# Row-half copies of weight differences on the compute engines, other stores from SyncE, and another order of a hand-ordered opening

## The chip, the cores and the metric

The kernel runs on one core of a Trainium2 chip. The metric is device microseconds of one execution; the median of five runs is quoted. A run is profiled separately, and every start time below is counted from the start of the profiled span of the kernel before.

The engines are named as in the profile: PE is TensorE, with PEld for its weight loads, DVE is VectorE, ACT is ScalarE, POOL is GpSimd and SP is SyncE. SP computes nothing here; it issues DMAs.

## The reference

There are two stages. The first is a dynamic convolution over time: each of 8 heads has 7 logits per position, a softmax turns them into weights, and each position's 192 features become the weighted sum of the last 7 positions' features. The second is a maxout layer over the 33,280 resulting rows.

```python
w = np.exp(weight_gen - weight_gen.max(-1, keepdims=True))     # (8, 4160, 8 heads, 7 taps)
w = w / (w.sum(-1, keepdims=True) + 1e-09)
out = np.einsum('bshk,bskhg->bshg', w, x_unf)                  # x_unf: 7 causal taps of x, zero padded
x = out.reshape(33280, 192)
g = np.maximum(x @ w1, x @ w2)                                 # w1, w2: (192, 1024)
return g @ w_out                                               # (1024, 192)
```

## The kernel before, in words

**The maths as the kernel does it.** Since max(a, b) = a + relu(b − a), the kernel forms d = w2 − w1 once, computes relu(x·d)·w_out on PE and adds x·(w1·w_out), where w1·w_out (tile `w10`, 192×192) is also formed once. The softmax is exp, a sum, a logarithm, a subtraction in place in the logits, and a second exp that writes the weights (`en_t`) in bf16.

**Tiling.** Each of the 128 partitions holds 260 consecutive positions, called columns. Columns come in batches of 16 (16 whole batches and one of 4). A batch is cut into units: the first batch into four units of 4 columns, the others into units of 8. DVE multiplies x by the weights (`mul`, L186, into `m_t`) and adds the seven taps (`add`, L203 and L208, into `y_t`). A DMA transpose issued by SP (L223) turns a unit's rows into features by tokens (`yt`). For the first two batches PE itself adds and transposes the taps (`tap_sums`, L261) and an engine copies the result to `yt` (`features`, L274). Then hidden tiles: 128 hidden features by 1024 tokens (`hid_tile`, L304: pairs of matmuls over 64 partition rows), relu to bf16 (`rd_t`, L318), and products with `w_out` into PSUM (`out_first`, L362, with `w10`; `out_hidden`, L350), a copy to `o_t` (`evac`, L406) and a store (L420).

**The weight differences.** The 192 feature rows are held as 128 rows (kind E) and two times 64 (kind T). Tile `wd` has three slots of 1024 columns. `diff` (L616, DVE, 128×512 each) writes E's difference in two halves, E0 and E1, and T's. A matmul of 64 rows needs its rows at the partitions of its token block, so each half also has to stand at the other 64 partitions: `cross` (L626) makes these six copies of 64×512 bf16 by SBUF-to-SBUF DMAs from SP: A0, B0 (of E0), A1, B1 (of E1), C0, C1 (of T). Hidden tiles 0, 1, 4, 5, 8, 9, … of the first units (features of E0) need A0, B0 and C0; tiles 2, 3, 6, 7, … need A1, B1 and C1.

**The opening.** What happens until hidden tile 32 is written out by hand as a list of steps, the string `ORDER` (L769). A step's engine gets its instructions in the order of the list, so each engine's queue is the list cut down to that engine's steps. The names: `exp.c`, `red.c`, `ln.c`, `sub.c`, `en.c` are the softmax of the columns from c on (exp, ln, en on ACT; red and sub on DVE); `mul.c`, `add.c.i` are DVE's; `taps.v.i` are PE's tap sums of four columns and `yt.v` their copy; `hid.t` is a hidden tile on PE and `relu.t` its relu; `out.u.i`, `more.u.i` are the two halves of four columns' output products on PE, `go.u` an empty ACT instruction between them that waits for the first half; `evac.u` is the copy to `o_t` and, for a unit's last columns, the store. `w1.E0`, `w1.E1`, `w1.T` cast w1 to bf16; `w1t` (PE) transposes it, `w1f` copies the transpose out of PSUM, `w10` (PE) multiplies it by w_out, `w10c` copies that. `/v` after a step gives it DVE's copy instead of ACT's. `load.*` are DMA issues, from POOL for x (`load_x`, with `after`, a tiny POOL copy that waits for a tile, as a gate) and, for `load.E1` and `load.wg1`, from SP. `move.32` is the first DMA transpose.

**Buffers around it.** Hidden tiles use two PSUM buffers in turn, the tap sums and output products two more. `rd_t` has seven buffers, one per pair of hidden tiles, handed out in the order of the first relu of each pair. `m_t` is one buffer.

**The steady stage.** From hidden tile 32 on, PE takes groups of three tiles (`hidden`, L469), ACT follows with relus and copies, and `extra` (L792) hangs the softmax and DVE work of later batches beside the tiles: ACT's queue holds `exp`, `ln` and `en` of the coming batches between its relus; DVE's holds, per batch, `mul` and three `add`s for each half, with `sub` of the next batch and `red` of the one after between them.

**Stores.** Units 0 to 5 (columns 0 to 31) are stored by DMAs issued from ACT's queue (L412), the rest from SP's.

Of the kernel before, what the change touches and what calls it, by code (L numbers as in the profile page):

```python
# [23 lines left out]
def kernel(  # L24
# [24 lines left out]
    BATCHES = [(c, min(16, CPP - c)) for c in range(0, CPP, 16)]  # L49
# [12 lines left out]
    UNITS = []  # L62
# [4 lines left out]
    SUMMED = sum(b < 2 for b, _, _ in UNITS)  # L67
# [34 lines left out]
    def load_wg(b, eng):  # L102
        c0, n = BATCHES[b]
        wg_ts[b] = pwg.tile([P, n * WGC], FP32, name="wg_t", tag="wg")
        eng.dma_start(
            out=wg_ts[b],
            in_=bass.AP(tensor=weight_gen.tensor, offset=c0 * WGC,
                        ap=[[CPP * WGC, P], [1, n * WGC]]),
        )
# [165 lines left out]
             in_=_sub(yps_ts[v], 0, [[512, 2], [64, 6], [1, 64]]))  # L275


    rd_at, hd_at, op_at, o_t = {}, {}, {}, []
    BLOCK = ((0, 1, 2), (1, 0, 2))
    HF = F // 2  # L280
    SYNC = mybir.DependencyInfo(mybir.DependencyClass.Sync, mybir.DependencyReason.DATA)
# [106 lines left out]
    def evac(p, n):  # L388

        tile_, at = op_at[p]  # L390
        o = o_t[0]
        if p == NT // 2 - 1:

            for j, copy, eng in ((0, nc.scalar.copy, nc.scalar), (1, nc.vector.tensor_copy, nc.sync)):
                c = place(p)[0] + 2 * j
                copy(out=o[:, c % 24 * D:(c % 24 + 1) * D], in_=tile_[:, at + j * 512:at + j * 512 + D])  # L396
                eng.dma_start(
                    out=bass.AP(tensor=out.tensor, offset=c * D, ap=[[CPP * D, P], [1, D]]),
                    in_=o[:, c % 24 * D:(c % 24 + 1) * D],
                )  # L400
            return
        runs = [[q for q in range(p, p + n) if column(2 * q)[0] == u]
                for u in range(column(2 * p)[0], column(2 * (p + n - 1))[0] + 1)]
        for qs in runs:
            c, h = place(qs[0])
            nc.scalar.copy(out=_sub(o, c % 24 * D, [[D, len(qs)], [h * D, 2], [1, D]]),  # L406
                           in_=_sub(tile_, at + (qs[0] - p) * D, [[D, len(qs)], [512, 2], [1, D]]))
        for q in range(p, p + n):
            u, i, _ = column(2 * q)
            if u < NU - 1 and i == UNITS[u][2] // 2 - 1:  # L410
                b, at_, n_ = UNITS[u]
                stores = [(nc.scalar if u < SUMMED else nc.sync, BATCHES[b][0] + at_, [1, n_ * D])]  # L412
            elif u == NU - 1:
                stores = [(nc.sync, place(q)[0], [2 * D, 2], [1, D])]
            else:
                continue
            for store in stores:

                def issue(eng=store[0], c=store[1], ap=store[2:], o=o):
                    eng.dma_start(  # L420
                        out=bass.AP(tensor=out.tensor, offset=c * D, ap=[[CPP * D, P], *ap]),
                        in_=_sub(o, c % 24 * D, ap),
                    )

# [12 lines left out]
    OUTS, c = [], 24  # L437
# [6 lines left out]
    NU = len(UNITS)  # L444
# [82 lines left out]
    w1 = {kind: pstage.tile([P, w], BF16, name="w1" + kind) for kind, w in (("E", F), ("T", HF))}  # L527
    w1t = pstage.tile([P, FCH * 2 * P], BF16, name="w1t")
# [49 lines left out]
    def after(tile_, at=0):  # L578
# [9 lines left out]
        out=wo[:, :].rearrange("p (f d) -> p f d", d=D),  # L588
        in_=bass.AP(tensor=moe_w_out.tensor, offset=0, ap=[[D, P], [P * D, FCH], [1, D]]),
# [26 lines left out]
        nc.vector.tensor_tensor(out=wd[:, to:to + HF], in0=ws[kind, 1][:, frm], in1=ws[kind, 0][:, frm],  # L616
                                op=ALU.subtract)

    def cross(part, h):

        slot = F + h * HF
        to, frm, col, src = {"A": (0, 64, slot, slot - F), "B": (64, 0, slot, slot - F),
                             "C": (64 * (1 - h), 64 * h, 2 * F + h * HF, 2 * F)}[part]
        if part == "C":
            col = 2 * F + HF
        nc.sync.dma_start(out=wd[to:to + 64, col:col + HF], in_=wd[frm:frm + 64, src:src + HF])  # L626

    def cast_w1(kind, h, copy):

# [73 lines left out]
    def evac_results(u):  # L703
# [7 lines left out]
    steps = {  # L711
        "warm": lambda c: warm(),
        "mask.0": lambda c: masked(0, 3, False), "mask.3": lambda c: masked(3, 6, True),
        "load.E1": lambda c: load_w("E", 1), "load.wg1": lambda c: load_wg(1, nc.sync),
        "load.wg2": lambda c: (after(yt_ts[1]), load_wg(2, nc.gpsimd)), "load.wg3": lambda c: load_wg(3, nc.gpsimd),
        "load.wg4": lambda c: load_wg(4, nc.gpsimd),
        "load.x24": lambda c: load_x(1, 8, 4), "load.x28": lambda c: (after(yt_ts[2]), load_x(1, 12, 4)),
        "load.x32": lambda c: load_x(2, 0, 4), "load.x36": lambda c: (after(yt_ts[3]), load_x(2, 4, 4)),
        "load.x40": lambda c: (after(yt_ts[4]), load_x(2, 8, 4)), "load.x44": lambda c: load_x(2, 12, 4),
# [20 lines left out]
    for b in range(4):  # L740
        for o, n in pieces(b):
            c = 16 * b + o
# [22 lines left out]
    for t in range(AHEAD):  # L765
# [1 line left out]
        steps[f"relu.{t}"] = lambda c, t=t: pair_relu(t, c is nc.vector.tensor_copy)  # L767

    ORDER = """  # L769
        exp.0 warm red.0 ln.0 sub.0 en.0.1 en.0.0 mask.0 mask.3 mul.0.0 cast.0 exp.4 mul.0.1 taps.0.0 red.4  # L770
        taps.0.1 diff.E0 ln.4 sub.4 cross.A0 cross.B0 load.E1 diff.T en.4.0 en.4.1 mul.4.0 cross.C0 cross.C1
        load.wg1 exp.8 yt.0 red.8 w1.T/v ln.8 w1.E0 sub.8 hid.1 en.8 taps.1.0 diff.E1 w1.E1 mul.4.1 cross.A1
        cross.B1 relu.1 w1t en.12 mul.8 taps.1.1 exp.16 hid.2 yt.1 hid.3 relu.2 red.16 taps.2.0 relu.3 hid.4
        w1f/v ln.16 hid.0 relu.4 taps.2.1 mul.12 relu.0 hid.7 w10 yt.2 load.wg2 relu.7 hid.11 sub.16 w10c
        taps.3.0 load.x24 hid.5 relu.11/v taps.3.1 en.20 out.0.0 en.16 relu.5/v taps.3.2 load.x28 hid.9 exp.32
        mul.16 hid.10 relu.9 out.0.1 relu.10 load.wg3 hid.6 taps.3.3 en.24 hid.8 yt.3/v go.0 relu.6 load.x32
        more.0.0 mul.20 taps.4.0 relu.8 taps.4.1 hid.14 en.28 taps.4.2 load.x36 more.0.1 exp.48 taps.4.3 hid.12
        evac.0 red.32 yt.4 taps.5.0 load.wg4 red.48 taps.5.1 ln.32 out.1.0 relu.14 sub.32 out.1.1 load.x40
        relu.12 mul.28 hid.13 go.1 en.32 taps.5.2 more.1.0 relu.13 load.x44 taps.5.3 hid.15 yt.5 more.1.1 mul.24
        load.x48 relu.15 out.2.0 hid.16 ln.48 evac.1 hid.18 relu.16 out.2.1 mul.32 relu.18 taps.6.0 hid.19  # L780
        taps.6.1 go.2 relu.19 hid.20 more.2.0 relu.20 taps.6.2 more.2.1 taps.6.3 evac.2 hid.23 yt.6 taps.7.0
        hid.21 sub.48.0 exp.64 add.32.0 taps.7.1 out.3.0 relu.21 taps.7.2 out.3.1 relu.23 sub.48.2 taps.7.3 go.3
        hid.22 add.32.1 yt.7 more.3.0 relu.22 hid.17 red.64.0 hid.25 relu.17 sub.48.1 more.3.1 red.64.1 en.40
        out.5.0 add.32.2 relu.25 hid.30 mul.40 move.32 out.5.1 evac.3 hid.31 go.5 relu.30 more.5.0 relu.31
        hid.28 out.4.0 relu.28 hid.24 out.4.1 relu.24 hid.26 add.40.0 go.4 en.48 more.4.0 more.5.1 relu.26
        more.4.1 add.40.1 ln.64 hid.29 evac.4 evac.5 add.40.2 hid.27 relu.27 en.56 relu.29
    """
    for step in ORDER.split():
        name, _, eng = step.partition("/")
# [63 lines left out]
```

## Time and profile before

| what | value |
|---|---|
| median of five runs | 430.9 us (430.04 to 431.5) |
| the profiled execution: its own time | 430.9 us |
| its span | 429.0 us (1.9 us lie around it) |
| PE, DVE, ACT, POOL busy | 401.2, 372.4, 355.9, 83.3 us |
| mean granted PE clock | 0.982 |
| first relu (L318 on ACT) | 20.88 us |
| DVE starts `mul` of columns 48 to 55 | 79.34 us |
| PE starts hidden tile 32 | 82.81 us |
| six `cross` DMAs, 64 KB each, median from issue to landing | 5.8 us |

How to read it: the span runs from the first to the last instruction. A busy engine need not be the limit; the chain of waits tells which work ended last, followed back. Rows of a timeline give start, duration, engine, line and operation, the tile written and the tiles read, the shapes, and in square brackets how long the engine sat idle before it and what ended that. Rows of instructions of one engine overlap a little in time (a relu row of 1024 elements lasts 1.02 us, but the next one starts 0.91 us after it).

### The profile page before, as it was taken

Reading aid. Unit: us, or ns where it says so; the run is one execution under the profiler, and the core shown is the slowest. Engines: PE = TensorE matmul, PEld = TensorE weight load, DVE = VectorE, ACT = ScalarE, POOL = GpSimd, SP = SyncE. Lnnn points to the kernel's source line nnn. Section 1 sums busy time; section 2 is a strip of 40 time slices with the busy share of each in tenths; the row PEclk is TensorE's granted clock in tenths of the full one; section 3 lists DMA queues with packets and bytes.
Section 4 is the critical chain, followed back from the end, with each engine's and each line's share of the span. In section 5 each row is a group of like instructions: output and inputs, shape, how many; then the busy total and the mean of one; then the engine's idle time right before and its main releaser. Section 6 shows DMA issues by size and latency. Waiting matters only on the chain.

```text
span 429.0 us, 16002 instructions
## 1 busy us (share of the span) xinstructions
PE 401.2 (94%) x7352; PEld 315.5 (74%) x7352; DVE 372.4 (87%) x219; ACT 355.9 (83%) x420; POOL 83.3 (19%) x111
## 2 busy tenths in 40 slices
PE   7289899699999999999999999999999999989984
PEld 3178777377777777777787778777777777767784
DVE  5675997999899999999999999999999999996000
ACT  4479878589998989998999899898998889688861
POOL 1313304021121212101212222221012222210000
PEclk9689999899999999999999999999999999999999
DMA  8864653768658667756765964765796396454113
GB/s 236 190 156 110 139 141 76 191 102 169 163 116 223 164 106 237 190 107 145 202 182 100 259 164 86 240 173 118 106 271 145 73 251 148 86 185 131 76 75 112
DMA packets 61296, 65.88 MB, mean 154 GB/s; under 512 B 47759, under 2 KB 50319, under 8 KB 61230
## 3 DMA queue, kind: packets, MB, share of 16 engines
q1 hardware_dynamic: 51376, 37.32, 31.8%
q0 software_dynamic: 8816, 24.24, 28.4%
q10 hardware_dynamic: 1038, 3.31, 2.1%
q8 instruction: 57, 0.93, 0.9%
q14 instruction: 9, 0.07, 0.1%
HBM read 35.96 MB, written 25.56 MB: 143 GB/s over the span
## 4 chain that ended last, share of the span: by engine, by line
PE 41%; DVE 40%; ACT 10%; issue 4%; DMA 3%; SPq 1%; ACTq 0%; DVEq 0%
DVE m_t L186 20%; PE op_ps L350 18%; PE hd L304 15%; DVE m_t L203 14%; ACT rd_t L318 6%; PE op_ps L362 4%; PE hdp L304 3%; DVE sum_t L142 2%; DVE wg_t L152 2%; DVE y_t L208 2%; DMA wd<-wd 2%; ACT en_t L170 1%; ACT o_t L406 1%; DMA ws1E<-in_moe_w_dram 1%; PE yps L261 1%
## 5 line engine op out<-in xcount | busy, mean ns | idle before, releaser
L318 ACT ACTIVATE rd_t<-hd 128x1024 bf16<-128x1024 f32 (+1 forms) x191 | 219.1, 1192 | 31.3 <-PE hd L304 30.1
L350 PE MATMUL op_ps<-wo,rd_t 64*128 64x192 bf16 x4160 | 210.6, 243 | 0.0
L186 DVE TENSOR_TENSOR m_t<-xb_t,en_t 128x10752 bf16<-128x10752 bf16 (+3 forms) x39 | 187.6, 4819 | 9.5 <-ACT en_t L170 8.6
L350 PEld LDWEIGHTS <-rd_t 64*128 64x128 bf16 x4160 | 181.1, 94 | 16.0
L304 PE MATMUL hd<-yt,wd 64*128 64x512 bf16 (+1 forms) x1392 | 176.2, 374 | 4.6 <-ACT rd_t L318 4.6
L304 PEld LDWEIGHTS <-wd 64*128 64x128 bf16 x1680 | 89.4, 94 | 60.7 <-issue 11.2
L203 DVE TENSOR_TENSOR m_t<-m_t 128x4608 bf16<-128x4608 bf16 (+3 forms) x58 | 122.8, 2117 | 0.2
L231 POOL CAST gate<-yt 128x1 f32<-128x1 bf16 x29 | 42.0, 1448 | 272.6 <-DMA yt<-y_t 272.6
L406 ACT COPY o_t<-op_ps 128x384 f32<-128x384 f32 (+1 forms) x94 | 56.3, 611 | 11.2 <-PE op_ps L350 11.0
L362 PE MATMUL op_ps<-w,yt 64*128 64x192 bf16 x780 | 55.9, 244 | 3.6 <-ACT o_t L406 3.0
L362 PEld LDWEIGHTS <-yt 64*128 64x128 bf16 x780 | 38.8, 94 | 21.6 <-issue 6.6
L318 ACT ACTIVATE rd_t<-hdp 128x1024 bf16<-128x1024 f32 x32 | 31.8, 1025 | 9.2 <-PE hdp L304 7.3
L170 ACT ACTIVATE en_t<-wg_t 128x896 bf16<-128x896 f32 (+4 forms) x49 | 35.8, 758 | 4.3 <-DVE wg_t L152 3.6
L304 PE MATMUL hdp<-yt,wd 64*128 64x256 bf16 (+1 forms) x288 | 28.2, 309 | 10.5 <-DMA wd<-wd 6.7
L208 DVE TENSOR_TENSOR y_t<-m_t 128x1536 bf16<-128x1536 bf16 (+1 forms) x29 | 27.3, 941 | 0.5
L396 DVE COPY o_t<-op_ps 128x192 f32<-128x192 f32 x1 | 0.4, 357 | 31.2 <-ACT o_t L396 31.2
L152 DVE TENSOR_TENSOR wg_t<-wg_t,sum_t 128x280 f32<-128x280 f32 (+6 forms) x47 | 22.3, 475 | 2.8 <-ACT sum_t L147 2.8
L142 DVE TENSOR_REDUCE sum_t<-e_t 128x64 f32<-128x448 f32 (+3 forms) x32 | 19.8, 620 | 1.8 <-ACT e_t L130 1.8
L115 POOL DMA_DIRECT2D xb_t<-in_x_dram x37 | 19.9, 537 | 7.2 <-DVE m_t L186 5.7
L130 ACT ACTIVATE e_t<-wg_t 128x896 f32<-128x896 f32 (+2 forms) x19 | 16.1, 849 | 1.4 <-DMA wg_t<-in_weight_gen_dram 1.3
L261 PE MATMUL yps<-ident,m_t 64*128 64x64 bf16 x672 | 16.0, 195 | 1.0 <-issue 0.9
L261 PEld LDWEIGHTS <-m_t 64*128 64x128 bf16 x672 | 14.9, 97 | 2.6 <-issue 1.6
(41 smaller groups left out, 62.5 us busy)
## 6 DMA issues: line engine op xcount, KB each, us to landing
out_dram<-o_t SPq DMA_DIRECT2D x28, 768.0 KB, 5.1
xb_t<-in_x_dram POOLq DMA_DIRECT2D x27, 384.0 KB, 4.9
wg_t<-in_weight_gen_dram POOLq DMA_DIRECT2D x14, 448.0 KB, 5.6
xb_t<-xb_t POOLq DMA_DIRECT2D x16, 288.0 KB, 5.4
xb_t<-in_x_dram POOLq DMA_DIRECT2D x10, 192.0 KB, 5.2
out_dram<-o_t ACTq DMA_DIRECT2D x4, 384.0 KB, 4.2
out_dram<-o_t ACTq DMA_DIRECT2D x2, 768.0 KB, 6.5
ws0E<-in_moe_w_dram SPq DMA_DIRECT2D x2, 256.0 KB, 4.2
```

The source lines that it names most:

```text
L152: nc.vector.tensor_tensor(out=w_t, in0=w_t, in1=_sub(s_ts[b], hs.start, [[1, hs.stop - hs.start], [0, K]]), op=ALU.subtract)
L170: nc.scalar.activation(out=_sub(en_ts[b], (o * WGC + (J * k0 + j * (k1 - k0)) * N) * 2, [[2 * N, k1 - k0], [2, N], [1, 2]]), in_=_sub(wg_t ...
L186: nc.vector.tensor_tensor(out=m_out, in0=x_in, in1=_sub(en_ts[b], (o * WGC + k0 * n * H) * 2, [[2, (k1 - k0) * n * H], [0, G // 2], [1, 2] ...
L203: nc.vector.tensor_tensor(out=to, in0=to, in1=taps(b, o, at, step, cnt), op=ALU.add)
L208: nc.vector.tensor_tensor(out=_sub(y_ts[b], o * D, [[64, 2], [P, 3 * w // 2], [1, 64]]), in0=taps(b, o, 0, 1, 1), in1=taps(b, o, 2, 1, 1), ...
L231: nc.gpsimd.tensor_copy(out=gate, in_=yt[:, 0:1])
L261: nc.tensor.matmul(yps_ts[v][:, r * 512 + k * 64:r * 512 + (k + 1) * 64], lhsT=m_t[half(r), at:at + P], rhs=ident[half(r), half(r)], start ...
L304: nc.tensor.matmul(hid_out(t, f, j), lhsT=wd[half(j), at:at + P], rhs=_sub(yt_ts[u][half(j), :], BLOCK[j][s] * P, [[3 * P, w // P], [1, P] ...
L318: nc.scalar.activation(out=rd[:, k * 1024:(k + n) * 1024], in_=hd[:, at:at + n * 1024], func=AF.Relu)
L350: return nc.tensor.matmul(op_out(c), lhsT=rd[half(r), k * 1024 + at:k * 1024 + at + P], rhs=wo[half(r), f * D:(f + 1) * D], start=False, s ...
L362: nc.tensor.matmul(op_out(c + j), lhsT=yt_ts[u][half(j), (3 * i + BLOCK[j][s]) * P:(3 * i + BLOCK[j][s] + 1) * P], rhs=w10[half(j), s * D: ...
L406: nc.scalar.copy(out=_sub(o, c % 24 * D, [[D, len(qs)], [h * D, 2], [1, D]]), in_=_sub(tile_, at + (qs[0] - p) * D, [[D, len(qs)], [512, 2 ...
```

## The change

Six things are edited:

- `cross` takes the step's copy, so the six row-half copies are instructions of ACT (A0, C0) and DVE (B0, C1, B1, A1) instead of DMAs from SP.
- The loads of E1 (two DMAs of 256 KB) and of the second batch's logits (448 KB) are no longer steps: SP issues them at once behind its other first loads.
- The stores of units 0 to 5 are issued by SP.
- A unit is stored once all its columns are copied out (`done` counts them), so the order of its evacuations is free.
- `w1.T` and `w1f` move from DVE to ACT, `w1.E1` from ACT to DVE.
- `ORDER` is another one. In it, for instance, `hid.0` comes first, `mul.4.1` stands before `mul.4.0`, `mul.20` before `mul.16`, the tap sums of unit 5 before those of unit 4, `en.40` 24 steps earlier, `evac.5` before `evac.4`, and `en.48` and `en.56` last.

```diff
-            if u < NU - 1 and i == UNITS[u][2] // 2 - 1:
+            done[u] = done.get(u, 0) + 1
+            if u < NU - 1 and done[u] == UNITS[u][2] // 2:
                 b, at_, n_ = UNITS[u]
-                stores = [(nc.scalar if u < SUMMED else nc.sync, BATCHES[b][0] + at_, [1, n_ * D])]
+                stores = [(nc.sync, BATCHES[b][0] + at_, [1, n_ * D])]
...
     load_logits(8, 8)
+    load_w("E", 1)
+    load_wg(1, nc.sync)
...
-    def cross(part, h):
+    def cross(part, h, copy):
...
-        nc.sync.dma_start(out=wd[to:to + 64, col:col + HF], in_=wd[frm:frm + 64, src:src + HF])
+        copy(out=wd[to:to + 64, col:col + HF], in_=wd[frm:frm + 64, src:src + HF])
...
-        "load.E1": lambda c: load_w("E", 1), "load.wg1": lambda c: load_wg(1, nc.sync),
...
-            steps[f"cross.{k}{h}"] = lambda c, k=k, h=h: cross(k, h)
+            steps[f"cross.{k}{h}"] = lambda c, k=k, h=h: cross(k, h, c)
...
-        exp.0 warm red.0 ln.0 sub.0 en.0.1 en.0.0 mask.0 mask.3 mul.0.0 cast.0 exp.4 mul.0.1 taps.0.0 red.4
-        taps.0.1 diff.E0 ln.4 sub.4 cross.A0 cross.B0 load.E1 diff.T en.4.0 en.4.1 mul.4.0 cross.C0 cross.C1
-        load.wg1 exp.8 yt.0 red.8 w1.T/v ln.8 w1.E0 sub.8 hid.1 en.8 taps.1.0 diff.E1 w1.E1 mul.4.1 cross.A1
-        cross.B1 relu.1 w1t en.12 mul.8 taps.1.1 exp.16 hid.2 yt.1 hid.3 relu.2 red.16 taps.2.0 relu.3 hid.4
-        w1f/v ln.16 hid.0 relu.4 taps.2.1 mul.12 relu.0 hid.7 w10 yt.2 load.wg2 relu.7 hid.11 sub.16 w10c
-        taps.3.0 load.x24 hid.5 relu.11/v taps.3.1 en.20 out.0.0 en.16 relu.5/v taps.3.2 load.x28 hid.9 exp.32
-        mul.16 hid.10 relu.9 out.0.1 relu.10 load.wg3 hid.6 taps.3.3 en.24 hid.8 yt.3/v go.0 relu.6 load.x32
-        more.0.0 mul.20 taps.4.0 relu.8 taps.4.1 hid.14 en.28 taps.4.2 load.x36 more.0.1 exp.48 taps.4.3 hid.12
...
-        hid.22 add.32.1 yt.7 more.3.0 relu.22 hid.17 red.64.0 hid.25 relu.17 sub.48.1 more.3.1 red.64.1 en.40
-        out.5.0 add.32.2 relu.25 hid.30 mul.40 move.32 out.5.1 evac.3 hid.31 go.5 relu.30 more.5.0 relu.31
-        hid.28 out.4.0 relu.28 hid.24 out.4.1 relu.24 hid.26 add.40.0 go.4 en.48 more.4.0 more.5.1 relu.26
-        more.4.1 add.40.1 ln.64 hid.29 evac.4 evac.5 add.40.2 hid.27 relu.27 en.56 relu.29
+        exp.0 warm red.0 ln.0 sub.0 en.0.1 en.0.0 mask.0 mask.3 mul.0.0 cast.0 exp.4 mul.0.1 w1.E0 taps.0.0
+        red.4 taps.0.1 diff.E0 ln.4 sub.4 cross.A0 cross.B0/v diff.T en.4.1 en.4.0 mul.4.1 exp.8 yt.0 cross.C0
+        red.8 w1.T hid.0 mul.4.0 ln.8 hid.1 relu.0 sub.8 taps.1.0 relu.1 w1.E1/v taps.1.1 diff.E1 en.8 w1t
+        cross.C1/v cross.B1/v yt.1 cross.A1/v mul.8 hid.2 exp.16 hid.4 relu.2 en.12 hid.7 red.16 w1f taps.2.0
+        taps.2.1 mul.12 ln.16 w10 yt.2 relu.4 load.wg2 w10c sub.16 taps.3.0 hid.3 load.x24 taps.3.1 relu.7/v
+        en.20 taps.3.2 relu.3 taps.3.3 mul.20 hid.5 hid.11 relu.5 load.x28 out.0.0 relu.11 hid.9 exp.32 yt.3/v
+        hid.8 load.wg3 out.0.1 relu.9 relu.8/v taps.5.0 load.x32 en.16 hid.6 red.32 go.0 taps.5.1 en.28 hid.15
+        relu.6/v en.24 more.0.0 relu.15 load.x36 taps.5.2 mul.16 more.0.1 ln.32 hid.14 exp.48 taps.5.3 hid.13
...
+        taps.7.0 relu.22 out.2.0 exp.64 taps.7.1 out.2.1 relu.17 hid.18 taps.7.2 go.2 ln.48 more.2.0 en.40
+        add.32.0 taps.7.3 more.2.1 yt.7 hid.19 relu.18 out.3.0 relu.19 sub.48.0 hid.23 add.32.1 out.3.1 evac.2
+        hid.16 go.3 relu.23 sub.48.1 more.3.0 sub.48.2 relu.16 mul.40 hid.31 more.3.1 relu.31 out.5.0 evac.3
+        hid.25 hid.29 relu.25 out.4.0 relu.29 out.5.1 hid.28 go.5 add.32.2 hid.24 relu.28 more.5.0 red.64.0
+        move.32 relu.24 add.40.0 hid.30 more.5.1 relu.30 hid.27 evac.5 out.4.1 add.40.1 hid.26 go.4 relu.27
+        more.4.0 relu.26 more.4.1 red.64.1 evac.4 add.40.2 ln.64 en.48 en.56
```

More of the change, by code (lines that the diff above doesn't have):

```diff
@@ L275, in features @@
              in_=_sub(yps_ts[v], 0, [[512, 2], [64, 6], [1, 64]]))
-    rd_at, hd_at, op_at, o_t = {}, {}, {}, []
+    rd_at, hd_at, op_at, o_t, done = {}, {}, {}, [], {}
     BLOCK = ((0, 1, 2), (1, 0, 2))
@@ L775 @@
-        taps.3.0 load.x24 hid.5 relu.11/v taps.3.1 en.20 out.0.0 en.16 relu.5/v taps.3.2 load.x28 hid.9 exp.32
-        mul.16 hid.10 relu.9 out.0.1 relu.10 load.wg3 hid.6 taps.3.3 en.24 hid.8 yt.3/v go.0 relu.6 load.x32
-        more.0.0 mul.20 taps.4.0 relu.8 taps.4.1 hid.14 en.28 taps.4.2 load.x36 more.0.1 exp.48 taps.4.3 hid.12
-        evac.0 red.32 yt.4 taps.5.0 load.wg4 red.48 taps.5.1 ln.32 out.1.0 relu.14 sub.32 out.1.1 load.x40
-        relu.12 mul.28 hid.13 go.1 en.32 taps.5.2 more.1.0 relu.13 load.x44 taps.5.3 hid.15 yt.5 more.1.1 mul.24
@@ L780 @@
-        load.x48 relu.15 out.2.0 hid.16 ln.48 evac.1 hid.18 relu.16 out.2.1 mul.32 relu.18 taps.6.0 hid.19
-        taps.6.1 go.2 relu.19 hid.20 more.2.0 relu.20 taps.6.2 more.2.1 taps.6.3 evac.2 hid.23 yt.6 taps.7.0
-        hid.21 sub.48.0 exp.64 add.32.0 taps.7.1 out.3.0 relu.21 taps.7.2 out.3.1 relu.23 sub.48.2 taps.7.3 go.3
-        hid.22 add.32.1 yt.7 more.3.0 relu.22 hid.17 red.64.0 hid.25 relu.17 sub.48.1 more.3.1 red.64.1 en.40
-        out.5.0 add.32.2 relu.25 hid.30 mul.40 move.32 out.5.1 evac.3 hid.31 go.5 relu.30 more.5.0 relu.31
@@ new lines @@
+        evac.0 load.wg4 yt.5 sub.32 taps.4.0 taps.4.1 relu.13 out.1.0 mul.24 relu.14 taps.4.2 taps.4.3 out.1.1
+        yt.4 en.32 hid.21 load.x40 red.48 hid.20 go.1 relu.21 more.1.0 mul.28 taps.6.0 relu.20 load.x44 load.x48
+        hid.10 more.1.1 relu.10 taps.6.1 hid.12 evac.1 mul.32 taps.6.2 relu.12 hid.22 taps.6.3 hid.17 yt.6
+        taps.7.0 relu.22 out.2.0 exp.64 taps.7.1 out.2.1 relu.17 hid.18 taps.7.2 go.2 ln.48 more.2.0 en.40
+        add.32.0 taps.7.3 more.2.1 yt.7 hid.19 relu.18 out.3.0 relu.19 sub.48.0 hid.23 add.32.1 out.3.1 evac.2
```

## The prediction

> **What bounds the kernel now.** I read the table by stretches first. From 83 to 374 us, PE and DVE are both full; before that neither is.
>
> ```profile
> 10.00:20.00 10.00, 1.99 (x60) 1.27 (x57) 6.20 (x11) 4.34 (x12) 3.35 (x5) 0.71 0.87 176
> 20.00:30.00 10.00, 8.71 (x229) 7.61 (x227) 9.65 (x7) 6.24 (x10) 1.81 (x4) 0.78 0.89 210
> 30.00:82.80 52.80, 46.13 (x1151) 39.29 (x1144) 43.15 (x23) 45.48 (x61) 13.73 (x16) 1.00 0.52 127
> ...
> 200.00:374.00 174.00, 173.46 (x3012) 135.22 (x3008) 173.76 (x96) 155.80 (x173) 38.78 (x44) 1.00 0.67 163
> ```
>
> The columns are the stretch, its length, then busy us of PE, PEld, DVE, ACT, POOL, and at the end the granted clock, DMA share and GB/s. The edits all lie in the first 83 us (the store rule aside), so the question is how much earlier the steady stage can start, and which engine's earlier start counts. The chain of waits answers the second part:
>
> ```profile
> 13.56 4.88 DMA ws1E<-in_moe_w_dram
> 18.54 0.70 DVE wd L616
> 19.77 6.44 DMA wd<-wd
> 26.26 0.73 PE hdp L304 x9
> ...
> 199.90 5.74 DVE m_t L186
> ...
> 374.92 0.28 DVE wg_t L152
> 375.20 0.02 issue
> 375.22 0.62 ACT en_t L170
> ```
>
> Early, the chain waits for E1's load and its crossing copy. From 200 us to 375 it is DVE. A DVE batch (`mul`, `add`s, `red`, `sub`) recurs every 23.66 us (199.90, 223.56, 247.22); PE needs 8.6 us per six hidden tiles (379.88, 388.46, 397.10), so about 22.9 for a batch's 16. DVE is slower by 0.75 per batch and eats a lead that it has at first. The DVE and ACT timelines show the lead at both ends:
>
> ```profile
> 79.34 5.75 DVE L186 TENSOR_TENSOR m_t<-xb_t,en_t 128x10752 bf16<-128x10752 bf16 x1
> ...
> 110.88 0.45 DVE L152 TENSOR_TENSOR wg_t<-wg_t,sum_t 128x280 f32<-128x280 f32 x1 [2.13 <-ACT sum_t L147]
> ...
> 85.66 1.88 ACT L318 ACTIVATE rd_t<-hd 128x2048 bf16<-128x2048 f32 x1 [2.90 <-PE hd L304]
> ...
> 375.22 0.62 ACT L170 ACTIVATE en_t<-wg_t 128x448 bf16<-128x448 f32 x1 [2.27 <-DVE wg_t L152]
> ```
>
> After 79.34 DVE idles once, 2.13 us, because ACT's `ln` came late (110.48); then never until its work is over. At 375.22 ACT waits 2.27 us for DVE and PE loses 1.43 (next product at 377.49). So the rule I use: **gain = (how much earlier DVE starts `mul` of columns 48 on, against 79.34) + 2.13, if ACT enters its steady stage at least 2.13 us more ahead than DVE does**; and at most 1.43 more than PE's gain. A still earlier PE only waits for DVE sooner.
>
> **The change, part by part.**
>
> *First hidden tile.* Before, relu.1 starts at 20.88, after C0 landed at about 19.8. New: ACT ends `exp.4` at 8.05, then `w1.E0` 0.61 (row L631), `ln.4` 10.43 as before, then A0 once diff.E0 is done (10.31 + 0.68 = 10.99). No row shows a 64×512 bf16 copy. On ACT the bounds are 0.31 (the 64×192 copy L671) and 1.02 (a 1024-element relu); nearest is the 128×512 cast, 0.61, taken as 0.6. On DVE they are 0.08 (L573) and 0.69 (L616); nearest its 128×512 cast, 0.41, taken as 0.4. Then four small `en` 0.89, `exp.8` 0.56, `yt.0` 0.77, C0 0.6: C0 is done at 10.99 + 0.6 + 0.89 + 0.56 + 0.77 + 0.6 = 14.4. The seven matmuls of hid.0 from the first that needs C0 on took 1.03 at half clock (19.81, same place). relu.0 starts near **15.4**, 5.5 us earlier.
>
> [...]
>
> *ACT from there to the steady stage.* From relu.1 (20.88) to the end of relu.29 (82.77) ACT spent 61.9 us: 2.1 in five store issues with their gaps, 7.9 in waits (1.37, 1.51, 0.93, 0.40, 0.59, 0.31, 0.81, 0.23, 0.17, 0.53, 1.01), so 51.9 of work. The new list from relu.0 on has the same work, without the stores, plus `en.8` (0.6) and `w1f`, two PSUM copies of 1024 elements (between 0.68, DVE's row L652, and 1.02, the relu; taken as 0.92, relus back to back): 51.9 + 0.6 + 1.8 = 54.3. `w1.T` comes before relu.0 and is in time for C0; `w1.E1` leaves. The `/v` behind relus adds nothing: the page has all 32 opening relus on ACT although the old list marks two. So `en.56`, now last, ends at 15.4 + 54.3 = 69.7 plus waits.
>
> *Waits.* (a) PE is cold: it idled 2.38 before 13.41 and the clock fell to 0.5 until about 24. The new gap is about 3 us (11.0 to 13.8), so I leave hid.1 and the tap sums of unit 1 at half clock; relu.1, `yt.1` and relu.2 come late by 0.4, 0.6 and 0.7: 1.7. (b) A new wait: `rd_t`'s seven buffers go round, and relu.27's pair takes the buffer of tiles 20 and 21, which `more.4.1` reads last. relu.27 stands right behind `go.4`, while PE still has hid.26 (0.65), `more.4.0` (0.66) and twelve of sixteen matmuls (0.5) to do: about 2. Behind it on ACT stand relu.26, `evac.4`, `ln.64`, `en.48`, `en.56`, and DVE waits for `en.48`. The old list had the same wait, 1.01 at 76.89. (c) The old small waits after 48 us, 3.8 together; I keep 3.3. Sum 7.0. Then `en.56` ends at 76.7 and `en.48` 0.93 before it, at **75.8**.
>
> [...] If the new gap spared the clock, (a) would fall and the sum would be 1.7 better.
>
> *DVE.* It idled 13.6 us from 10 to 79.34 (3.76, 0.35, 5.68, 0.90, 2.91). It loses `w1.T` and `w1f` (1.7), gains `w1.E1` and four copies (2.0). With no wait it would reach `mul.48` at 66.0. Waits that I find by following both queues: about 0.5 for x columns 4 to 7 before `mul.4.1`, 2.7 for `en.20` before `mul.20`, 1.3 for `en.16`: 70.5. The old waits for E1's load (3.76) and `en.40` (2.91) go: E1 is issued near 7 and, by 4.2 to 5.8 us to landing, there by 13; `en.40` now stands far ahead. What is late next is `en.48`, so DVE starts at 75.8 and its own copies cost nothing; without that cover they would cost 1.6.
>
> *SP and POOL.* SP issues E1 and the logits of batch 1 behind the first logits (6.47), each held until an earlier load has landed, as that one was (0.4 us); 12 to 14 us was nearly free on the DMA engines (share 0.28). POOL keeps its list. SP's stores wait for `evac` in front of the transposes: `evac.3` near 61, `move.32` after `add.32.2`, `evac.4` near 74, while transposes take 3.7 and hidden tile 40 comes 11 us after tile 32. Hidden. The freed issue slots on ACT are in the sum.
>
> **Sum.** DVE starts 79.34 − 75.8 = 3.5 earlier. ACT's first steady relu comes at 76.7 instead of 85.66, 9.0 earlier, 5.5 more than DVE, so the 2.13 goes too. Gain 5.6. The profiled execution took 430.9 (429.0 span and 1.9 around it), which is also the median of the five runs: **425.3**.
>
> **Rivals.**
>
> - *Few waits.* If (c) is almost nothing and PE keeps its clock, waits are 3, `en.48` comes at 71.8, gain 7.5 + 2.1: 421.3. For it: an order with slack at many places. Against: the old ACT queue had 3.8 us of small waits, and three engines are within 5 us of full.
> - *The gain stays in the opening.* Waits of 9 to 11 because PE, ACT and DVE are coupled at each tile: `en.48` at 78 to 80, gain 1.5 to 3.5: about 428. For it: the old run had 7.9 in a stretch that began later, with fuller queues; single PE issue gaps of 0.8 to 0.9 stand at 49 and 60.
> - *Slower: columns 4 to 7 of x.* `mul.4.1` now stands before `mul.4.0` and needs a load that landed at 12.43, beside 960 KB of transfers newly put early. `red.8`, `ln.8` and, behind `ln.8` on ACT, every relu wait for it, so each us late costs one. The gain is used up when it lands 5.6 us late, near 18, that is 11.4 us after its issue; the longest `xb_t` landing early on is 10.2, the median 5.7. At 20 us: 432.5.
> - *It does not do what it says* holds only for the relus' `/v`, counted above.
>
> **How the numbers follow.** Forecast (423.5 to 427) 0.50; few waits 0.17; gain left in the opening 0.20; within 0.2% (0.86 us, about what a measurement of this kernel can tell from no change) 0.05; slower 0.08. Faster is 0.50 + 0.17 + 0.20 = 0.87. The range runs from 420.8, below the few-waits time, to 429.5, the end of the second rival, and leaves out some 0.15.
>
> **What would show it.** Right: first relu near 15 to 16; no DMA `wd<-wd`; DVE starting `mul` of 10752 elements for columns 48 on near 76, having waited for ACT's `en_t`; no 2.13 wait at the first steady `ln`; several waits of ACT for DVE (`sum_t` or `wg_t`) in the second half. Wrong: `mul.4.1` waiting for x; DVE reaching `mul.48` after 79; or ACT never waiting for DVE later, which would make PE the bound and the whole ACT lead the gain.

## The result, and the profile after

The changed kernel takes **428.36 us** (median of 31 runs, 425.95 to 431.4) where the kernel before takes 430.85 (52 runs beside them): ratio 0.9947, 95% interval 0.9931 to 0.9963. It is faster by 2.5 us; 5.6 were forecast. The profiled execution took 428.66 us, with a span of 426.8. Executions of one kernel differ by some us, so times are compared by medians, and the ratios leave out an execution that took over 1.5% longer than the kernel's fastest.

The table by stretches of the changed kernel (columns as in the prediction):

```profile
10.00:20.00 10.00, 6.36 (x160) 4.91 (x152) 8.17 (x14) 7.28 (x16) 4.20 (x5) 0.66 0.77 179
20.00:30.00 10.00, 7.01 (x216) 6.24 (x215) 7.48 (x4) 7.71 (x14) 4.96 (x8) 1.00 0.91 175
30.00:78.90 48.90, 44.23 (x1080) 37.79 (x1073) 39.32 (x21) 42.03 (x56) 8.32 (x13) 1.00 0.49 121
...
200.00:374.00 174.00, 170.31 (x2948) 132.41 (x2945) 173.76 (x99) 152.51 (x169) 35.12 (x44) 1.00 0.68 163
```

From 10 to 20 us PE does 6.36 us of work instead of 1.99: the hidden tiles do begin earlier. From 20 to 30 PE does less than before (7.01 against 8.71), at a higher clock (1.00 against 0.78): it stands still for part of that time. From 30 to 78.9 ACT's 42.03 is just what the kernel before has in the same stretch; the lead won early is not enlarged there. From 200 to 374 DVE's busy time is 173.76 in both kernels.

The chain of waits of the changed kernel has no `wd<-wd` DMA any more. It goes through ACT in front of DVE's product of columns 48 on, and then along DVE:

```profile
6.52 7.00 DMA xb_t<-in_x_dram
17.22 2.37 PE yps L261 x64
24.34 2.53 issue
...
78.01 0.91 ACT en_t L170
78.95 5.76 DVE m_t L186
85.07 2.47 DVE m_t L203
90.85 5.67 DVE m_t L186
```

The first line is the load of x that `mul.4.1` needs, the third a standstill of PE that the prediction did not have. The timelines of DVE and ACT at the same two places as before:

```profile
78.95 5.76 DVE L186 TENSOR_TENSOR m_t<-xb_t,en_t 128x10752 bf16<-128x10752 bf16 x1 [6.47 <-ACT en_t L170]
...
77.89 1.94 ACT L170 ACTIVATE en_t<-wg_t 128x896 bf16<-128x896 f32 x2
79.72 2.80 ACT L318 ACTIVATE rd_t<-hd 128x2048 bf16<-128x2048 f32 x2
...
372.61 0.62 ACT L170 ACTIVATE en_t<-wg_t 128x448 bf16<-128x448 f32 x1 [2.26 <-DVE wg_t L152]
```

DVE starts the product at 78.95, only 0.39 us earlier than before, after waiting 6.47 us for `en.48`. After that it never waits until its work is over: the 2.13 us wait for `ln` is gone. ACT's steady relus start at 79.72 instead of 85.66, and late in the run ACT waits 2.26 us for DVE, as before. It is the last of seven such waits after 150 us; the kernel before has two. DVE is still the bound. The rule of the prediction, gain = earlier start + 2.13, gives 0.39 + 2.13 = 2.5, which is the measured gain.

The same rule can be written as a sum: span = DVE's start of `mul.48` + DVE's later idle time + a constant. The constant is 347.5 in the kernel before (429.0 − 79.34 − 2.13) and 347.9 in the changed one.

### The profile page after: what moved, and what is told of

It reads as the page before. It is cut to its first block, busy times and chain, and to the rows that moved or that the text cites. A ratio compares the mean times of both kernels' runs of the same rounds, so it can differ in the third digit from the quotient of the medians.

```text
span 426.8 us, 16015 instructions
## 1 busy us (share of the span) xinstructions
PE 399.1 (94%) x7352; PEld 314.7 (74%) x7352; DVE 372.2 (87%) x221; ACT 358.4 (84%) x424; POOL 78.5 (18%) x111
## 4 chain that ended last, share of the span: by engine, by line
DVE 66%; PE 20%; issue 5%; ACT 5%; DMA 3%; SPq 0%; DVEq 0%; POOL 0%; ACTq 0%
DVE m_t L186 34%; DVE m_t L203 24%; PE op_ps L350 9%; PE hdp L304 4%; PE hd L304 4%; DVE sum_t L142 3%; DVE y_t L208 3%; DVE wg_t L152 3%; ACT rd_t L318 2%; PE yps L261 2%; PE op_ps L362 2%; DMA xb_t<-in_x_dram 2%; DMA xs<-in_x_dram 1%; ACT o_t L406 1%; ACT en_t L170 1%
## 5 line engine op out<-in xcount | busy, mean ns | idle before, releaser
L231 POOL CAST gate<-yt 128x1 f32<-128x1 bf16 x29 | 34.7, 1197 | 277.7 <-DMA yt<-y_t 277.7
L304 PE MATMUL hdp<-yt,wd 64*128 64x256 bf16 (+1 forms) x288 | 27.2, 317 | 4.6 <-ACT yt L274 3.2
L261 PE MATMUL yps<-ident,m_t 64*128 64x64 bf16 x672 | 14.8, 196 | 5.6 <-issue 3.8
L261 PEld LDWEIGHTS <-m_t 64*128 64x128 bf16 x672 | 13.7, 99 | 7.8 <-issue 5.6
```

Source lines behind the costliest of these rows:

```text
L231: nc.gpsimd.tensor_copy(out=gate, in_=yt[:, 0:1])
L261: nc.tensor.matmul(yps_ts[v][:, r * 512 + k * 64:r * 512 + (k + 1) * 64], lhsT=m_t[half(r), at:at + P], rhs=ident[half(r), half(r)], start ...
L304: nc.tensor.matmul(hid_out(t, f, j), lhsT=wd[half(j), at:at + P], rhs=_sub(yt_ts[u][half(j), :], BLOCK[j][s] * P, [[3 * P, w // P], [1, P] ...
```

## The experiments

The theory that the runs were to test: the steady stage is DVE's, so the time follows from when DVE starts `mul.48`; that start is set by `en.48`, which stands last on ACT's queue; and ACT's waits in the opening are longer than forecast. The rivals were that PE's or ACT's own lead counts, that the new order or the stores bring the gain and not the copies, and that the transfers set the opening's pace. Each expectation names its own pair, A and B. All times are in us; the ratio is to the kernel before. The third column adds up ACT's waits between the first relu and the start of `mul.48`. A profile shows one execution, whose own time is its span and 1.9 us: 429.57 in e1, 434.32 in e10, 430.67 in e6, 431.69 in e5, 431.07 in e8 and 431.02 in e9, which is 2 to 6 us above the median of that kernel.

| kernel | first relu | ACT's waits | start of mul.48 | later idle of DVE | span | median | ratio (95%) |
|---|---|---|---|---|---|---|---|
| before | 20.88 | – | 79.34 | 2.13 | 429.0 | 430.85 | 1 |
| changed | 16.10 | 9.97 | 78.95 | 0 | 426.8 | 428.36 | 0.9947 (0.9931–0.9963) |
| e1 en.48 earlier | 16.22 | 3.91 | 70.49 | 8.96 | 427.7 | 424.05 | 0.9843 (0.9808–0.9878) |
| e11 the same again | 16.28 | 5.79 | 71.57 | 3.16 | 422.7 | 426.57 | 0.9907 (0.9877–0.9937) |
| e1b en.56 earlier too | 15.50 | 6.02 | 70.81 | 2.99 | 421.9 | 425.89 | 0.9857 (0.9801–0.9913) |
| e2 eight `rd_t` | 15.85 | 8.42 | 77.16 | 0 | 425.0 | 426.91 | 0.989 (0.9834–0.9945) |
| e7 mul.4.0 first | 15.22 | 9.48 | 77.66 | 0 | 425.5 | 427.07 | 0.9912 (0.9879–0.9946) |
| e4 crossing by DMA | 17.70 | 15.37 | 86.11 | 0 | 433.5 | 436.15 | 1.0119 (1.0075–1.0164) |
| e6 old order | 16.73 | 11.15 | 77.15 | 3.62 | 428.8 | 427.66 | 0.994 (0.9908–0.9972) |
| e5 stores from ACT | 17.24 | 11.56 | 81.97 | 0 | 429.8 | 429.49 | 0.9958 (0.9926–0.999) |
| e3 a load of x later | 16.98 | 8.34 | 78.39 | 0 | 426.2 | 428.07 | 0.994 (0.9911–0.9968) |
| e8 logits earlier | 15.89 | 12.52 | 81.37 | 0 | 429.2 | 428.44 | 0.9947 (0.9923–0.9971) |
| e9 e1 + e2 + e7 | 15.16 | 7.93 | 72.03 | 8.90 | 429.1 | 428.86 | 0.9945 (0.9914–0.9975) |
| e10 e1 without gates | 17.26 | 7.31 | 74.22 | 10.39 | 432.6 | 429.49 | 0.9937 (0.9903–0.9971) |

In all fourteen profiles the span less the start less the idle time is 347.4 to 348.3 us. That is the firmest thing that the study shows: everything in this case is told by the start of one DVE instruction and by what DVE waits after it; the work that follows is the same in all. Start and waits differ between executions of the same kernel, though: the changed kernel's runs spread over 5.4 us, and e1 and e11, one kernel, have 8.96 and 3.16 us of later idle. So a single profile explains its own execution, and the median says what the edit is worth.

### e1, e11 and e1b: en.48 from the end of the queue to the middle

```diff
-        ... relu.25 out.4.0 relu.29 out.5.1 hid.28 ...
+        ... relu.25 out.4.0 relu.29 en.48 out.5.1 hid.28 ...
-        ... add.40.2 ln.64 en.48 en.56
+        ... add.40.2 ln.64 en.56
```

e11 is e1 word for word; e1b moves `en.56` as well:

```diff
-        ... add.40.1 hid.26 go.4 relu.27
-        more.4.0 relu.26 more.4.1 red.64.1 evac.4 add.40.2 ln.64 en.56
+        ... add.40.1 hid.26 go.4 en.56 relu.27
+        more.4.0 relu.26 more.4.1 red.64.1 evac.4 add.40.2 ln.64
```

> Edit: only the step en.48 is moved, from last but one to just behind relu.29, where ACT idled 1.11 us in the changed kernel. Theory A (the end is set by when DVE starts the product of columns 48 on, which waits 6.47 us for en.48 behind the relu that waits for its rd_t buffer): DVE starts near 72.5 instead of 78.95; then DVE is ahead of ACT and idles again some 3 us at the first steady ln, so the net gain is ACT's own lead, 85.66 - 79.72 = 5.9: about 424.9 us, ratio 0.986 to before. Theory B (PE, not DVE, sets the end of the changed kernel, so the late en.48 is harmless): no change from the changed kernel, 428.4, ratio 0.9947.

> Edit: en.48 behind relu.29 as in the run before, and en.56 behind go.4, in front of relu.27, where ACT waited 2.04 us for the rd_t buffer. Theory A (with en.48 out of the way ACT's own entry into the steady stage is the limit): ACT's last opening step ends about 1 us earlier, DVE still starts columns 48 on near 72.5 or before, and the time falls by up to 1 us more: 423 to 424, ratio 0.982 to 0.984. Theory B (DVE is now held by x loads, which the run before showed once at columns 64 on, 3.16 us for a copy of the halo): no further gain, 424 to 425.

> e1 again, word for word the same kernel, beside the one above on the same chip. Theory A (the gain is real and comes from the earlier start of mul.48, less what DVE then waits): DVE starts near 70.5 us, span = start + later idle + 347.4 to 348.3, median 423 to 425.5. Theory B (six runs were too few, the times spread between 424 and 431 because waits for loads come and go): median 426 to 428, with idle time after the start of 6 us or more in the profile.

DVE and ACT in e1:

```profile
65.32 1.03 ACT L170 ACTIVATE en_t<-wg_t 128x896 bf16<-128x896 f32 x1
...
70.49 5.75 DVE L186 TENSOR_TENSOR m_t<-xb_t,en_t 128x10752 bf16<-128x10752 bf16 x1
...
97.39 5.76 DVE L186 TENSOR_TENSOR m_t<-xb_t,en_t 128x10752 bf16<-128x10752 bf16 x1 [3.16 <-DMA xb_t<-xb_t]
```

`en.48` is ready at 66.4, and DVE starts the product at 70.49 with no wait. The prediction had 70.5 for DVE left to itself; that it comes out so exactly is luck, for DVE waited 5.2 us on the way where 4.5 were forecast, and had 0.7 less work. The 8.5 us come back to DVE, but not all to the time. In this execution DVE is so far ahead that it waits for loads of x (the 3.16 above), and ACT for logits; in e11 it waits 1.03 for x and 2.13 for ACT's `ln`. The twelve runs of this kernel together have a median of 425.6. So the place of `en.48` costs the changed kernel 1.8 to 4.3 us (by the two medians), and theory B of e1, that PE sets the end and the late `en.48` is harmless, fell. e11's own two theories are both half right: the idle time is small, as in A, and the median is that of B. e1 is the best version found. Moving `en.56` too brings nothing more that these runs can tell from e1 (six runs, 423.5 to 432.7); its profile has the shortest span of all, which one execution alone does not prove.

### e4, e6 and e5: the parts of the change by themselves

e4 puts the crossing back on DMAs, e6 takes the old list of steps, without its loads and with `/v` for the copies that DVE makes, and e5 puts the first columns' stores back on ACT.

```diff
-        copy(out=wd[to:to + 64, col:col + HF], in_=wd[frm:frm + 64, src:src + HF])
+        nc.sync.dma_start(out=wd[to:to + 64, col:col + HF], in_=wd[frm:frm + 64, src:src + HF])
```

```diff
-        ... mul.0.1 w1.E0 taps.0.0
+        ... mul.0.1 taps.0.0 red.4
+        taps.0.1 diff.E0 ln.4 sub.4 cross.A0 cross.B0/v diff.T en.4.0 en.4.1 mul.4.0 cross.C0 cross.C1/v
+        exp.8 yt.0 red.8 w1.T/v ln.8 w1.E0 sub.8 hid.1 en.8 taps.1.0 diff.E1 w1.E1 mul.4.1 cross.A1/v
...
```

```diff
-                stores = [(nc.sync, ...)]
+                stores = [(nc.scalar if u < SUMMED else nc.sync, ...)]
```

> Edit: the changed kernel with the six row-half copies by DMAs from SP again, at their new places. Theory A (the direct copies are what starts the hidden tiles early): A0 and B0 land about 5.8 us after their issue near 11.5, C0 near 20, so the first relu comes at 19.5 to 20.5 instead of 16.10; half of that is still seen at en.48, which ends near 81: 430.5, ratio 0.999 to before. Theory B (waits later in the opening swallow the earlier start whole, so the copies bring nothing): 428.4, ratio 0.9947.

> Edit: the changed kernel with the list of steps of the kernel before (the two load steps taken out, B0, C1, B1 and A1 marked for DVE); copies, early loads and stores from SP stay. Theory A (the copies and loads bring the start forward, and the new list gives most of it back through en.48 standing last): first relu near 16, DVE reaches the product of columns 48 on near 75, some 4 us earlier than 79.34, and the time is 425.5 to 427.5, below the changed kernel. Theory B (the new list is what brings the gain): 430 or more, at most 1 us below before.

> Edit: the changed kernel with the stores of units 0 to 5 issued from ACT's queue again. Theory A (the slots are worth their count): four of them lie before en.48, 0.42 us each, so DVE starts columns 48 on 1.7 us later, near 80.6, and the time is 430.1. Theory B (ACT waits for PE behind two of them and again 2.04 us before relu.27, so most of it is hidden): start 0 to 0.8 later, 428.4 to 429.2.

PE in e4:

```profile
16.22 2.72 PE L304 MATMUL hdp<-yt,wd 64*128 64x256 bf16 x22 [2.58 <-DMA wd<-wd]
28.04 3.83 PE L304 MATMUL hdp<-yt,wd 64*128 64x256 bf16 x34 [6.30 <-DMA wd<-wd]
```

With DMAs PE waits for `wd` twice, 8.9 us in all, and SP's issues of the six copies stretch from 10.86 over 10.18 us; the second wait ends at 28.04, 7.0 us after the last of these issues. The start comes 7.2 us later and the median 7.8: in the new order the copies are worth 7.8 us. The direction was expected, the size was not (430.5 by theory A), and the first relu came earlier than expected (17.70 against 19.5 to 20.5). What was missed is the second wait, of hidden tile 2 for E1's copies. The kernel before has that wait too, until 26.26 instead of 28.04, so why the new order with DMAs is 5 us slower than the kernel before is only in part explained.

e6 has the copies, the early loads and SP's stores in the old order, and its time cannot be told from that of the changed kernel (427.66 against 428.36, ratios 0.994 and 0.9947). In its profile, of an execution 3 us above the median, `mul.48` starts earlier (77.15) and 3.62 us go to waits of DVE for ACT later. So **the new order as such brings nothing, as far as these runs can tell, beyond the other edits**, and theory B (430 or more) fell. Which of the copies, the early loads and SP's stores makes the gain in the old order was not separated: no run has the old order with one of them alone. e5 is 1.1 us slower in the median, between what the two theories gave. Its interval overlaps with the changed kernel's, and its profile has the first relu 1.1 later too; how much of it is ACT's issue slots stays open.

### e2 and e7: single waits

```diff
-    prd = ctx.enter_context(tc.tile_pool(name="prd", bufs=7))
+    prd = ctx.enter_context(tc.tile_pool(name="prd", bufs=8))
```

```diff
-        ... en.4.1 en.4.0 mul.4.1 exp.8 yt.0 cross.C0
-        red.8 w1.T hid.0 mul.4.0 ln.8 ...
+        ... en.4.0 en.4.1 mul.4.0 exp.8 yt.0 cross.C0
+        red.8 w1.T hid.0 mul.4.1 ln.8 ...
```

> Edit: the changed kernel with eight rd_t buffers instead of seven, so that relu.27's pair need not wait for the product that reads tiles 20 and 21 last. Theory A (that wait is part of en.48's lateness): the 2.04 us wait goes, evac.4 then waits for its product for a part of it, en.48 ends 1.4 us earlier, DVE starts columns 48 on near 77.5: 427.0, ratio 0.991. Theory B (PE is as late anyway, and ACT waits for it at the next step): DVE starts within 0.3 us of 78.95, 428.4.

> Edit: the changed kernel with mul.4.0 and en.4.0 before mul.4.1 and en.4.1, as in the kernel before, so that DVE does not stand still for columns 4 to 7 of x. Theory A (each us of that wait is a us at the end, as the prediction's slower rival priced it): the first relu starts at 15.3 to 15.5 instead of 16.10, and DVE starts columns 48 on 0.7 earlier: 427.7. Theory B (later waits of ACT for PE swallow it): first relu earlier, start of columns 48 on within 0.3 us of 78.95, 428.4.

The wait of relu.27 for `rd_t`'s buffer, first in the changed kernel, then in e2:

```profile
75.18 1.94 ACT L318 ACTIVATE rd_t<-hdp 128x1024 bf16<-128x1024 f32 x2 [2.04 <-PE op_ps L350]
```

```profile
73.34 1.94 ACT L318 ACTIVATE rd_t<-hdp 128x1024 bf16<-128x1024 f32 x2 [0.58 <-PE op_ps L350]
```

An eighth buffer takes 1.5 us of the wait away, `mul.48` starts 1.8 earlier and the median falls by 1.45: a us in front of `en.48` is about a us of the time. e7 takes `mul.4.1`'s wait for x away; the first relu comes 0.9 earlier, the start 1.3, the median 1.3. The prediction's slower rival thus had its price about right (one for one), and its size was 0.8 us. Both were nearest to their theory A. The intervals of both (0.9834 to 0.9945 and 0.9879 to 0.9946) still overlap with the changed kernel's, so the gains rest on the starts in the profiles as much as on the medians.

### e3 and e8: the transfers early on

e3 issues the first load of x for columns 16 to 23 (384 KB) only behind `yt.1`; e8 issues batch 3's logits (448 KB) with the first loads.

```diff
-    load_x(1, 0, 8)
...
-        "load.wg2": lambda c: (after(yt_ts[1]), load_wg(2, nc.gpsimd)), ...
+        "load.wg2": lambda c: (after(yt_ts[1]), load_x(1, 0, 8), load_wg(2, nc.gpsimd)), ...
```

```diff
+    load_wg(3, nc.gpsimd)
...
-        ... "load.wg3": lambda c: load_wg(3, nc.gpsimd),
+        ... "load.wg3": lambda c: None,
```

> Edit: the load of columns 16 to 23 of x (768 KB read) goes out behind the gate on yt of unit 1, near 21 us, instead of near 17. In the changed kernel PE stood still for 2.53 us at 24.34 with nothing that the profile shows to wait for, and its one 16 KB instruction block of that stretch came at 24.48, with the DMA engines over full (share 1.05 to 1.24 from 20 to 26). Theory A (the block's fetch waits behind these loads): the block comes earlier, near 21 to 22, the PE gap falls below 1 us, ACT's wait for yt of unit 2 (2.23 us) falls to about 1, and the time by 0 to 1.5 us: 427 to 428.4. Theory B (the gap belongs to the instruction count, not to DMA traffic): the gap stays at 2 to 3 us, and the time at 428.4. Either way DVE should still wait for en.48.

> Edit: in the changed kernel the logits of batch 3 (448 KB) are loaded behind columns 16 to 23 of x, near 18 us, instead of near 36, so that the DMA engines have some 2 us more to move just when PE's 16 KB instruction block is due. Theory A (PE's standstill near 24 us is its block waiting among the loads): the block starts at 25 to 27, the gap grows to 3 to 4.5 us, and DVE starts columns 48 on 1 to 2 us later, 80 to 81: 429.5 to 430.5. Theory B (the block's time does not depend on the loads): block near 24, gap 1.9 to 2.5, start within 0.5 us of 78.95, 428.4.

Both were aimed at PE's standstill at 24 us. PE in the changed kernel (its two standstills, each in the brackets of the row that ends it), in e3 and in e8:

```profile
26.87 0.24 PE L261 MATMUL yps<-ident,m_t 64*128 64x64 bf16 x5 [2.53 <-issue]
...
57.02 0.32 PE L261 MATMUL yps<-ident,m_t 64*128 64x64 bf16 x9 [1.31 <-issue]
```

```profile
31.82 0.93 PE L304 MATMUL hdp<-yt,wd 64*128 64x256 bf16 x13 [1.76 <-issue]
```

```profile
26.90 0.24 PE L261 MATMUL yps<-ident,m_t 64*128 64x64 bf16 x5 [1.72 <-issue]
```

With the load later the standstill at 24 is gone, as theory A of e3 had it, but one of 1.76 comes at 30. In e8 the first is not longer but shorter, the second, at 57.78, is longer (2.08), and the start of `mul.48`, 81.37, is as late as theory A of e8 had it. The medians are those of the changed kernel. e8 is a weak test, though: POOL issued the extra load at 20.81 and not near 18, and the DMA engines' share from 16 to 24.4 us rose only from 1.00 to 1.06 (it is 0.77 in e3). So **whether traffic lengthens the standstill stays open**; the earlier logits and the later x are worth nothing that these runs can tell. What goes with the standstill is told in the last section.

### e9 and e10: what limits the earlier start

e9 puts e1, e2 and e7 together. e10 is e1 without the gate copies (L231) of the first four transposed units:

```diff
-        nc.gpsimd.tensor_copy(out=gate, in_=yt[:, 0:1])
+        if u >= 10:
+            nc.gpsimd.tensor_copy(out=gate, in_=yt[:, 0:1])
```

> Edit: the changed kernel with three things of earlier runs together: en.48 behind relu.29, eight rd_t buffers, mul.4.0 before mul.4.1. Theory A (DVE's start is set by DVE alone, near 71, and ACT's own entry, now some 2 us earlier, is what holds it at the first steady ln): gain over the run with en.48 early alone of 1.4 for the buffer and 0.7 for mul.4.0: 421.5 to 422.5, ratio 0.979 to 0.981. Theory B (x loads hold DVE at columns 64 on, since POOL's gate copies end late beside DVE's products): no better than that run, 424.

> The kernel with en.48 early (e1), and in addition the tiny POOL copies that gate the loads (L231) are left out for the first four transposed units (columns 32 to 63); nothing of the computation changes. Theory A: with DVE ahead, the gate copy of the first transposed unit stands beside DVE's product (6.20 us in e1, 0.25 in the changed kernel) and delays the loads of x behind it; without it DVE's idle time after its start of mul.48 falls from 8.96 us (e1's profile) to at most 3 and the time to 421 to 423. Theory B: the loads are late for another reason (buffers of x come free only with DVE's products, or the transfers collide with transposes and stores), so the idle time stays above 6 us and the time within 1 us of e1's repeat, or above it by 1 to 3 us because ungated loads meet the opening's transfers. By both DVE starts mul.48 at 70 to 73 us.

Three edits that each lowered the median do not add: e9's 428.86 is no better than the changed kernel, worse than e1, and missed by both theories (421.5 to 422.5, and 424). In the profiled execution, the slowest of the twelve, DVE starts at 72.03 and then idles 8.9 us, 3.85 of them for x and 5.05 for ACT. POOL beside DVE in e9:

```profile
83.21 6.43 POOL L231 CAST gate<-yt 128x1 f32<-128x1 bf16 x1 [10.76 <-DMA yt<-y_t]
89.58 0.53 POOL L115 DMA_DIRECT2D xb_t<-in_x_dram  x1
...
83.84 5.75 DVE L186 TENSOR_TENSOR m_t<-xb_t,en_t 128x10752 bf16<-128x10752 bf16 x1
```

A copy of one element per partition lasts 6.43 us and ends just when DVE's product beside it ends; the load of x stands behind it. It looked like the new bound. e10 takes it away, and **that theory fell**: later idle 10.39, median 429.49 against 426.57 for e11 on the same chip, where 421 to 423 were expected. PE and SP in e10, then SP, POOL and DVE in e11:

```profile
85.25 2.75 PE L305 MATMUL hd<-yt,wd 64*128 64x512 bf16 x12 [8.15 <-DMA yt<-y_t]
...
68.14 7.20 SPq L223 DMA_TRANSPOSE yt<-y_t  x1
```

```profile
65.50 1.58 SPq L223 DMA_TRANSPOSE yt<-y_t  x1
...
83.43 5.74 POOL L231 CAST gate<-yt 128x1 f32<-128x1 bf16 x1 [12.12 <-DMA yt<-y_t]
...
96.34 5.76 DVE L186 TENSOR_TENSOR m_t<-xb_t,en_t 128x10752 bf16<-128x10752 bf16 x1 [1.03 <-DMA xb_t<-xb_t]
```

Without the gate POOL issues four transfers between 67.54 and 69.69, over the transpose that SP issues at 68.14. That instruction now takes 7.20 us instead of 1.58, the two transposes of units 6 and 7 land 17.0 and 8.7 us after their issue, PE waits 8.15 us for the first, ACT 7.66 for PE, and DVE 6.39 and 4.00 for ACT. So in this execution, 4.8 us above e10's median, loads without a gate met the transposes. That the gates save more than they cost is not shown: the intervals of e10 and e11 overlap. e11 shows from the other side that the gate copy is not the bound: it lasts 5.74 us as well, and DVE waits only 1.03 for x. In e1b it lasts 5.49, and DVE never waits for x. What limits e9, and why its median is 3.3 us above that of e1 and e11 together, stays open.

## Why the forecast was right in its mechanism and too large in its size

- **What bounds the kernel: right.** DVE's start of `mul.48` plus the constant, in fourteen profiles. The 2.13 went as forecast, and ACT waits for DVE several times in the second half, 2.26 at the end.
- **First relu: 15.4 forecast, 16.10 measured.** The copies were right: DVE's first lasts 0.29 (0.4 taken), ACT's 0.62 (0.6 taken). The 0.7 is x: `mul.4.1` waits 0.83 for the load of columns 4 to 7. In e7, without that wait, the relu comes at 15.22. (The rival's time for x at 20 us should read 432.9: 7.6 us after 12.43, of which 5.6 use up the gain.)
- **ACT's work: right.** To `en.48`'s end the forecast had 54.3 − 0.93 = 53.4; measured, from the first relu to the start of `mul.48` less the waits, it is 52.9 (and 52.9 to 53.1 in e2, e3, e7 and e8, whose ACT has the same steps).
- **ACT's waits: this is the step that failed.** Forecast 7.0, measured 9.97. Wait (a), the cold PE, was 1.7 and is 1.01, at `yt.1`. Wait (b), for `rd_t`'s buffer, was about 2 and is 2.04. Wait (c), the small ones after 48 us, was 3.3 and is 4.69 (0.29, 0.24, 2.02, 0.53, 0.50, 1.11). In no term at all was the 2.23 at `yt.2`. That one and the 2.02 are both of ACT for tap sums that PE delivers late, behind its standstills of 2.53 and 1.31:

```profile
27.15 0.80 ACT L274 CAST yt<-yps 128x768 bf16<-128x768 f32 x1 [2.23 <-PE yps L261]
...
58.35 0.80 ACT L274 CAST yt<-yps 128x768 bf16<-128x768 f32 x1 [2.02 <-PE yps L261]
```

- **The sum.** The start came 78.95 − 75.8 = 3.15 late: 0.7 from the first relu, 3.0 from the waits, less 0.5 of work. Forecast gain 5.6 − 3.15 = 2.45; measured 2.5. This is the rival "the gain stays in the opening" (`en.48` at 78 to 80, about 428). I had its evidence in hand, the single issue gaps of 0.8 to 0.9 at 49 and 60 us in the profile before, and took the waits of a schedule whose queues were to be tighter at less than the 7.9 that the looser one had.
- **How much of it is PE's standstills** stays open: they stand right before the two waits, but e3, which has none at 24, has waits of 8.34, and e2, which has one of 1.92, has 8.42. A wait taken away at one tile partly comes back at another.
- **What I costed and the change left on the table:** `en.48` last. Its place was in the prediction (each wait before it delays DVE) and e1 prices it: 1.8 to 4.3 us.
- **The clock.** The new gap of PE is 3.16 us (forecast 3), and the granted clock is 0.50 from 13 to 18 us and 1.00 from 20 on; it was halved 1.9 us into the gap. So the gap did not spare the clock, the case that the prediction priced at 1.7. In e2, e5, e6, e9 and e10 the clock is 0.50 once more, for 3.4 us, from 0 to 1.5 us after PE's standstill near 24 (in e2 from 26.1 to 29.5); the changed kernel's is not. So the profiles differ in this too.

## What to carry to other kernels

In a hand-ordered opening, find the one instruction whose start sets the end (here a product on the engine that is full afterwards), follow its operand to the queue that makes it, and price each edit by that operand's time and by the waits that follow it. An operand that another engine needs early should not stand last behind work that has slack: moving one step was worth about as much as all the edits of the change. Where two edits each gain by letting an engine run ahead, measure them together, since the loads and the waits between engines that were hidden are the next to cost time (in e9 DVE idled 3.85 us for x and 5.05 for ACT).

## What the runs showed of the hardware

**PE's standstills ended 2.2 to 2.5 us after a block of instructions began.** The trace has a DMA queue of its own for instructions, with 57 packets of 16 KB in an execution. One of them in the changed kernel, from 24 to 26 us (packets, MB, share of 16 engines):

```profile
q8 instruction: 1, 0.02, 3.0%
```

By the start times of these packets in the trace it begins at 24.48, and PE's standstill ends at 26.87, 2.4 us later; the second begins at 54.62, and PE goes on at 57.02, again 2.4 later. All of PE's standstills of over 0.6 us that end between 20 and 64 us with no other cause, in the fourteen profiles, 23 of them, end 2.2 to 2.5 us after such a packet's start; in the kernel before they are the 0.88 at 50.03 (packet at 47.81) and the 0.80 at 60.76 (58.59). Counting PE's and PEld's instructions before the packet near 24 us sorts the profiles as well: where it begins after 454 to 532 of them (before, e1, e3, e4, e7, e11) PE has no standstill there of over 0.6 us, and where it begins after 662 to 705 (the changed kernel, e1b, e2, e5, e6, e8, e9, e10) PE stands still for 1.72 to 3.28 us. Whether PE was waiting for the block itself is not shown: no view shows instructions waiting. What makes a block start late was not found: in e3, with less traffic before it, it began at 22.41, in e8, with a little more, at 24.68, and no run changed the traffic alone.

**A tiny POOL copy lasted until DVE's product beside it ended.** It takes 6.43 us in e9, 6.20 in e1 and 5.74 in e11, where it lies beside a product of 5.75 and ends within 0.1 us of it; in the changed kernel, where it falls behind the product's end, the same copy takes 0.25. Why the copy lasts so long is not shown.

**A DMA transpose took longer with loads issued beside it:** 7.20 us on its queue in e10, with four transfers issued within 2.2 us, against 1.58 in e11. In e1 the one issued at 88.54, beside two transfers of POOL's (88.04 and 88.56), took 5.18. No run changed the loads alone.
